# Windowed attention and a four-expert layer on one core: steps ordered by a list scheduler, gate logits turned back by transposes

## The chip, the cores and the metric

The kernel runs on one core of a Trainium2 chip. A core has five engines that work side by side and wait for one another by semaphores: TensorE (PE in the profile; its weight loads are PEld), VectorE (DVE), ScalarE (ACT), GpSimd (POOL) and SyncE (SP), which here only starts DMA transfers. Each engine works through its own queue in the order of the program. The metric is device time in microseconds, the median of several runs; less is better.

## The reference

Eight batches of 576 positions. First a symmetric sliding-window attention with 8 heads of width 64, then a layer of four causal attention experts, of which each position uses the best two.

```
scores = q @ k.T / sqrt(64), kept where |i - j| <= 32
x = softmax(scores) @ v                      # heads side by side: 576 x 512
logits = x @ w_gate                          # 576 x 4
top 2 of 4, w = softmax over these two
for e in 4 experts:
    a = causal softmax((x @ wq[e]) @ (x @ wk[e]).T / sqrt(64))
    out += w[e] * (a @ (x @ wv[e]) @ wo[e])  # where e is among the two
```

## The kernel before

The work of a batch is cut into steps, each a Python function that issues a handful of instructions; all loops are unrolled. A window group `g` is four of the eight heads, so a batch has two groups.

- `load_qk`, `load_v`: DMAs from SP's queue. Per group 0.59 MB (576 KB) each of k and q; per batch 1.18 MB of v, and then two copies inside the chip (lines 94 and 95, 0.92 MB in all) that make a second, shifted layout of v. These copies wait in SP's queue until v has landed.
- `turn(b, g, nm)` (line 207): VectorE transposes k or q of a group, two instructions.
- `win_scores(b, g, half)` (228): 40 small fp32 products on TensorE into two PSUM tiles, then an exp on ScalarE (234) and a product with the mask (236), on VectorE in batch 0 and on GpSimd later.
- `win_av` (264) multiplies by v for a pair of heads, and ScalarE copies the result (268). `win_sums` (243) makes the softmax sums of a batch, and five VectorE instructions (248 to 253) invert them into `RS`. `win_norm` (279 to 283) spreads `RS` by four products, VectorE multiplies (281, tile XTF), GpSimd casts (283, tile XTB).
- `moe_gate1` (299, 302), `moe_gate2` (304 to 326) and `moe_gate3` (331 to 337): the gate. TensorE leaves the logits as partial sums in `GT`, in four groups of 32 rows; `moe_gate2` multiplies 128 columns of `GT` by a selection matrix `SELG`, which adds the four groups and turns the result, so that positions lie on partitions, in tile `pl`.
- `moe_proj_qk` (349, out by ScalarE at 354 for q and VectorE at 356 for k), `moe_proj_v` (371), `moe_scores(b, j, c)` (391, exp at 394, causal mask on GpSimd at 398 to 405), `moe_av` (417, VectorE 424 to 426), `moe_turn` (439), `moe_y` (450, ScalarE 455, DMA 457 and 459). Experts go in two pairs `j`; a pair's scores come in four chunks `c`.

PSUM has eight banks: three tiles of two banks (`slot`), which nearly all steps share, and two of one bank (`slot1`) for `sums`, `pl` and `pt`. SBUF tiles rotate as well: three of each of `kn` and `qn`, two of `vsb`, three of `AT` (the window weights of a group), one of `XTF` and `XTB`.

What sets the order is the table `ORDER`, written out by hand and run once per batch in a software pipeline: `N` steps work for the next batch but one round (loads, first turns), `W` for the batch of this round (window scores), `M` for the batch before it (all the rest up to the experts' products) and `Z` for the one before that (second pair's product, output). The program keeps this order on each engine.

## Time and profile before

| | |
|---|---|
| median of 3 runs | 350.93 us (347.72 to 351.21) |
| profiled execution, its own time | 351.94 us |
| its span, first to last instruction | 350.2 us |
| mean granted TensorE clock | 0.924 of full |
| busy: PE, PEld, DVE, ACT, POOL | 279.6, 206.9, 190.4, 148.6, 131.9 us |
| DMA | 48.00 MB, mean 137 GB/s |

The profiled execution's own time is 1.74 us above its span. In the rows further down a line such as `[12.37 <-DVE QKE L356]` says that the engine was idle 12.37 us before the instruction and that a VectorE instruction of line 356, which wrote tile QKE, ended that wait.

### The profile page before, as it was taken

Reading aid. Unit: us, or ns where it says so; the run is one execution under the profiler, and the core shown is the slowest. Engines: PE = TensorE matmul, PEld = TensorE weight load, DVE = VectorE, ACT = ScalarE, POOL = GpSimd, SP = SyncE. Lnnn points to the kernel's source line nnn. Section 1 sums busy time; section 2 is a strip of 40 time slices with the busy share of each in tenths; the row PEclk is TensorE's granted clock in tenths of the full one; section 3 lists DMA queues with packets and bytes.
Section 4 is the critical chain, followed back from the end, with each engine's and each line's share of the span. In section 5 each row is a group of like instructions: output and inputs, shape, how many; then the busy total and the mean of one; then the engine's idle time right before and its main releaser. Section 6 shows DMA issues by size and latency. Waiting matters only on the chain.

```text
span 350.2 us, 12556 instructions
## 1 busy us (share of the span) xinstructions
PE 279.6 (80%) x5672; PEld 206.9 (59%) x5680; DVE 190.4 (54%) x380; ACT 148.6 (42%) x224; POOL 131.9 (38%) x186
## 2 busy tenths in 40 slices
PE   0878609887997899797988798879979898869864
PEld 0766406576576756585757655766658566744541
DVE  7976035638483558537573749274853743370440
ACT  1235503441646255623554175515562266415332
POOL 7002700443348055615354354614561534530110
PEclk9999955798999999998999999998999699998886
DMA  7997897800588039720957077803972030003003
GB/s 283 221 220 189 150 303 184 232 4 2 184 225 236 10 127 266 142 118 3 321 120 211 4 247 179 226 2 135 264 154 101 2 137 2 4 2 135 2 1 135
DMA packets 58181, 48.00 MB, mean 137 GB/s; under 512 B 45584, under 2 KB 45584, under 8 KB 58128
## 3 DMA queue, kind: packets, MB, share of 16 engines
q1 hardware_dynamic: 58128, 47.20, 49.4%
q8 instruction: 44, 0.72, 0.9%
q14 instruction: 9, 0.07, 0.1%
HBM read 30.42 MB, written 9.44 MB: 114 GB/s over the span
## 4 chain that ended last, share of the span: by engine, by line
PE 62%; DVE 15%; ACT 9%; DMA 5%; SPq 4%; issue 3%; ACTq 0%; POOL 0%; POOLq 0%; DVEq 0%
PE sc L228 13%; PE u L264 9%; PE pp L349 8%; PE po L417 7%; PE py L450 7%; ACT ATE L394 5%; PE pv L371 5%; PE sums L243 4%; DVE XTF L281 4%; ACT AT L234 4%; DVE Tkn L207 3%; DMA kn<-in_k_dram 3%; PE pl L308 3%; PE ps L391 3%; PE pg L299 2%
## 5 line engine op out<-in xcount | busy, mean ns | idle before, releaser
L236 POOL TENSOR_TENSOR AT<-AT,MASKP 128x576 f32<-128x576 f32 x56 | 77.8, 1411 | 65.0 <-ACT AT L234 65.0
L228 PE MATMUL sc<-Tqn,Tkn 32*64 32x128 f32 (+3 forms) x2560 | 60.2, 302 | 19.0 <-DVE Tqn L207 8.3
L234 ACT ACTIVATE AT<-sc 128x576 f32<-128x576 f32 x64 | 38.2, 648 | 86.9 <-PE sc L228 86.9
L228 PEld LDWEIGHTS sc<-Tqn,Tkn 32*64 32x64 f32 x2560 | 50.4, 150 | 29.6 <-DVE Tqn L207 8.8
L394 ACT ACTIVATE ATE<-ps 128x1024 bf16<-128x1024 f32 x64 | 51.0, 836 | 36.1 <-PE ps L391 35.9
L283 POOL CAST XTB<-XTF 128x576 bf16<-128x576 f32 x32 | 21.3, 668 | 89.6 <-DVE XTF L281 89.6
L264 PE MATMUL u<-AT,vsb 128*64 128x64 f32 (+1 forms) x1024 | 39.2, 236 | 8.8 <-ACT ATE L394 6.8
L207 DVE STREAM_TRANSPOSE Tkn<-kn 128x576 f32<-128x576 f32 x32 | 37.3, 1240 | 15.4 <-DMA kn<-in_k_dram 15.4
L264 PEld LDWEIGHTS u<-AT,vsb 128*64 128x64 f32 x1024 | 35.5, 143 | 12.1 <-ACT ATE L394 7.6
L268 ACT COPY us<-u 128x576 f32<-128x576 f32 x32 | 20.5, 639 | 41.0 <-PE u L264 41.0
L207 DVE STREAM_TRANSPOSE Tqn<-qn 128x576 f32<-128x576 f32 x32 | 37.2, 1240 | 0.0
L391 PE MATMUL ps<-QKE 64*128 64x512 bf16 (+2 forms) x192 | 22.2, 290 | 16.9 <-DVE QKE L356 14.1
L356 DVE CAST QKE<-pp 128x576 bf16<-128x576 f32 x16 | 12.0, 747 | 43.0 <-PE pp L349 43.0
L398 POOL TENSOR_SCALAR_AFFINE_SELECT ATE<-ATE 128x384 bf16<-128x384 bf16 x32 | 16.0, 523 | 48.7 <-ACT ATE L394 48.7
L417 PE MATMUL po<-VE,ATE 128*128 128x65 bf16 (+2 forms) x480 | 27.1, 198 | 2.0 <-POOL ATE L398 1.6
L424 DVE RECIPROCAL po<-po 128x8 f32<-128x8 f32 (+1 forms) x32 | 6.2, 194 | 39.0 <-PE po L417 38.4
L455 ACT COPY ysb<-py 128x1024 f32<-128x1024 f32 (+1 forms) x24 | 19.6, 873 | 18.4 <-PE py L450 9.9
L450 PE MATMUL py<-WO,OTT 128*128 128x512 bf16 (+1 forms) x72 | 24.1, 461 | 3.2 <-DVE OTT L441 2.0
L417 PEld LDWEIGHTS <-ATE 128*128 128x128 bf16 (+2 forms) x480 | 21.4, 101 | 7.8 <-POOL ATE L398 1.7
L248 DVE RECIPROCAL sums<-sums 128x144 f32<-128x144 f32 x8 | 8.5, 1067 | 30.0 <-PE sums L243 30.0
L371 PE MATMUL pv<-WV,XTB 128*128 128x256 bf16 (+1 forms) x160 | 22.4, 292 | 2.4 <-ACT AT L234 2.4
L391 PEld LDWEIGHTS <-QKE 64*128 64x128 bf16 x192 | 7.0, 96 | 27.0 <-DVE QKE L356 15.1
(72 smaller groups left out, 333.2 us busy)
## 6 DMA issues: line engine op xcount, KB each, us to landing
kn<-in_k_dram SPq DMA_DIRECT2D x16, 576.0 KB, 6.3
qn<-in_q_dram SPq DMA_DIRECT2D x16, 576.0 KB, 6.9
vsb<-in_v_dram SPq DMA_DIRECT2D x32, 256.0 KB, 7.0
out_dram<-ysb SPq DMA_DIRECT2D x16, 512.0 KB, 2.9
vsb<-vsb SPq DMA_DIRECT2D x8, 512.0 KB, 5.1
vsb<-vsb SPq DMA_DIRECT2D x8, 384.0 KB, 7.0
vsb<-in_v_dram SPq DMA_DIRECT2D x8, 128.0 KB, 4.5
out_dram<-ysb SPq DMA_DIRECT2D x8, 128.0 KB, 3.4
```

Source lines behind the costliest of these rows:

```text
L207: nc.vector.transpose(T[:, dh, :].rearrange("p (t s) -> p s t", s=18), n_[:, :, 32 * dh:32 * dh + 32])
L228: nc.tensor.matmul(sl[hh // 2][64 * par:64 * par + 64, hh % 2, lo - c0:hi - c0], KT[r, dh, k0:k0 + 64], QT[r, dh, lo:hi], start=(dh == 0), ...
L234: nc.scalar.activation(ap, sl[p][:, :, 0:HS], EXP, scale=scale_att)
L236: eng.tensor_tensor(out=ap, in0=ap, in1=MASK[:, None, c0:c0 + HS].to_broadcast([128, 2, HS]), op=MULT)
L264: nc.tensor.matmul(u[64 * x:64 * x + 64, half, lo - HS * half:hi - HS * half], V[:, c, h, :], A[:, h % 4, lo:hi], start=True, stop=True, s ...
L283: nc.gpsimd.tensor_copy(XTB[:, pair, :], XTF[:, pair, :])
L349: nc.tensor.matmul(pp[:, half, 0:HS], WQK[j][n][:, dt, :], XTB[:, dt, HS * half:HS * half + HS], start=(dt == 0), stop=(dt == NDT - 1))
L371: nc.tensor.matmul(o, XTB[:, dt, 128 * t:128 * t + n], WV[:, dt, :], start=(dt == 0), stop=(dt == NDT - 1))
L391: nc.tensor.matmul(ps[0:rows, eo, at:at + hi - lo], QKE[r, 1, 128 * kt:128 * kt + nrow(kt)], QKE[r, 0, lo:hi], start=True, stop=True)
L394: nc.scalar.activation(ATE[0:rows, :, 512 * c:512 * c + w], ps[0:rows, :, 0:w], EXP, scale=scale_moe)
L417: nc.tensor.matmul(po[0:n, eo, 65 * qt:65 * qt + 65], ATE[0:nk, eo, o:o + n], VE[0:nk, kt, 2 * j + eo, :], start=(kt == 0), stop=(kt == qt))
L450: nc.tensor.matmul(py[0:n, t - t0, :], OTT[:, j, 128 * t:128 * t + n], WO[:, j, :], start=(j == 0), stop=(j == 1))
```

## The change

The hand-written table goes. In its place every step of all eight batches is declared with its engine costs, its predecessors (data and buffer reuse) and the PSUM tiles that it takes (`D` of the wide ones, `S` of the narrow). `way` is the longest way from a step to the end. A greedy loop keeps a clock per engine and repeatedly takes, of the steps whose predecessors are placed, the one with the smallest start time less 0.06 times its `way`; a step without TensorE work is placed as soon as its start is due. The program then issues the steps in that order. `load_qk` is split so that k and q are loaded by separate steps. In `moe_gate2` the five products with `SELG` become five fp32 transposes of `GT` into a wide PSUM tile `ptr`, and two VectorE reductions add the four groups.

```diff
-    def load_qk(b, g):
-        for nm, src in (("kn", k), ("qn", q)):
+    def load(b, g, nm):
+        for src in ({"kn": k, "qn": q}[nm],):
...
     def moe_gate2(b):
         sh = [128, NQT, 4]
+        ptr = slot("ptr")
+        for t in range(NQT):
+            nc.tensor.transpose(ptr[:, t // 4, 128 * (t % 4):128 * (t % 4) + 128],
+                                GT[:, 128 * t:128 * t + 128], ident)
         pl = slot1("pl")
-        for t in range(NQT):
-            nc.tensor.matmul(pl[:, 4 * t:4 * t + 4], GT[:, 128 * t:128 * t + 128], SELG,
-                             start=True, stop=True)
+        nc.vector.tensor_reduce(pl[:, 0:16].rearrange("p (t e) -> p t e", e=4),
+                                ptr[:, 0, :].rearrange("p (t d e) -> p t e d", d=4, e=32)[:, :, 0:4, :],
+                                axis=AXX, op=ADD)
+        nc.vector.tensor_reduce(pl[:, 16:20],
+                                ptr[:, 1, 0:128].rearrange("p (d e) -> p e d", e=32)[:, 0:4, :],
+                                axis=AXX, op=ADD)
...
-    ORDER = """
-        M win_av 0 | M win_av 1 | M win_sums | M win_av 2 | M win_av 3 | Z moe_av 1
...
-        M moe_gate1 | M moe_proj_qk 0 0 | M moe_proj_qk 0 1 | W turn 1 qn
...
-    """
+                if i > 2:
+                    step(("load", i, nm), lambda b=b, g=g, nm=nm: load(b, g, nm), 0,
+                         [("turn", i - 3, nm)], then=[("DMA", 1.6), ("LAT", 2.0)])
...
+        else:
+            step(("load_v", b), lambda: None, 0, [], then=[("LAT", 14.0)])
...
+        step(("G2", b), lambda b=b: moe_gate2(b), 0.55, [("G1", b)] + ([("G3", b - 1)] if b else []), D=1, S=1,
+             then=[("DVE", 1.7)])
...
+    def way(n):
+        if n not in tail:
+            s_ = steps[n]
+            tail[n] = s_["pe"] + sum(c + 0.2 for _, c in s_["then"]) + max([way(u) for u in users[n]], default=0)
+        return tail[n]
...
+    while left:
+        cand = [(try_step(n), n) for n in left if all(a in done for a in left[n]["after"])]
+        now = free["PE"]
+        best = None
+        for t, n in cand:
+            if not left[n]["pe"]:
+                ok = t <= now + 0.3
+                key = (0 if ok else 1, t if not ok else -way(n))
+            else:
+                key = (1, max(t, now) - SLACK * way(n) * 0.01)
+            if best is None or key < best[0]:
+                best = (key, t, n)
...
     with tc.manual_schedule():
-        load_qk(1, 0)
+        load(1, 0, "kn")
+        load(1, 0, "qn")
         load_weights(0)
...
+        for n in order:
+            steps[n]["fn"]()
+            if n == ("turn", 1, "qn"):
+                spread_sel(0)
```

What this makes of the order is shown at three places. The first is ScalarE's queue in batch 0, where the tiles `sc` are the window scores and `u` the products with v, in the order in which TensorE makes them. Before:

```order
L234 ACTIVATE AT_239<-sc0_294 128x2x288
L234 ACTIVATE AT_239<-sc1_295 128x2x288
L234 ACTIVATE AT_340<-sc0_341 128x2x288
L234 ACTIVATE AT_340<-sc1_342 128x2x288
L234 ACTIVATE AT_340<-sc0_391 128x2x288
L234 ACTIVATE AT_340<-sc1_392 128x2x288
L268 COPY us_454<-u_437 128x576
L268 COPY us_473<-u_456 128x576
```

After:

```order
L230 ACTIVATE AT_218<-sc0_267 128x2x288
L230 ACTIVATE AT_218<-sc1_268 128x2x288
L264 COPY us_340<-u_323 128x576
L264 COPY us_362<-u_345 128x576
L230 ACTIVATE AT_368<-sc0_369 128x2x288
L230 ACTIVATE AT_368<-sc1_370 128x2x288
L230 ACTIVATE AT_368<-sc0_415 128x2x288
L230 ACTIVATE AT_368<-sc1_416 128x2x288
```

The first group's two products with v (`us_340`, `us_362`) now stand ahead of the second group's scores (`AT_368`).

The second is SP's queue after the weights (`tmpw`, `tmpv` and `tmpo` are the experts' weights); `kn_387` and `qn_389` before are k and q of batch 1, group 1, and so are `kn_265` and `qn_313` after. Before:

```order
L179 DMA tmpv_216<-in_moe_wv_dram 128x4x64 x4
L183 DMA tmpo_221<-in_moe_wo_dram 64x512 x4
L90 DMA vsb_286<-in_v_dram 128x8x64 x4
L92 DMA vsb_286<-in_v_dram 64x8x64
L94 DMA vsb_286<-vsb_286 64x4x512
L95 DMA vsb_286<-vsb_286 64x3x512
L82 DMA kn_387<-in_k_dram 128x1152
L82 DMA qn_389<-in_q_dram 128x1152
L82 DMA kn_646<-in_k_dram 128x1152
```

After:

```order
L175 DMA tmpv_202<-in_moe_wv_dram 128x4x64 x4
L179 DMA tmpo_207<-in_moe_wo_dram 64x512 x4
L83 DMA kn_265<-in_k_dram 128x1152
L83 DMA qn_313<-in_q_dram 128x1152
L91 DMA vsb_315<-in_v_dram 128x8x64 x4
L93 DMA vsb_315<-in_v_dram 64x8x64
L95 DMA vsb_315<-vsb_315 64x4x512
L96 DMA vsb_315<-vsb_315 64x3x512
L83 DMA kn_461<-in_k_dram 128x1152
L83 DMA qn_463<-in_q_dram 128x1152
L83 DMA kn_569<-in_k_dram 128x1152
```

The k and q of that group now stand ahead of v of batch 1 (`vsb_315`) and its two copies; behind these come batch 2's `kn_461`, `qn_463` and `kn_569`.

The third is VectorE's queue where batch 1 is normalised. Before:

```order
L281 TENSOR_TENSOR XTF_1157<-us_1018,rb_1159 128x576
L281 TENSOR_TENSOR XTF_1157<-us_1037,rb_1166 128x576
L441 COPY OTT_1173<-pt_1174 128x576
L281 TENSOR_TENSOR XTF_1157<-us_1097,rb_1181 128x576
L281 TENSOR_TENSOR XTF_1157<-us_1116,rb_1188 128x576
L441 COPY OTT_1173<-pt_1195 128x576
L207 STREAM_TRANSPOSE Tkn_1202<-kn_887 128x18x32 x2
```

After:

```order
L381 CAST VE_659<-pv_1007 64x4x64
L203 STREAM_TRANSPOSE Tqn_1051<-qn_657 128x18x32 x2
L277 TENSOR_TENSOR XTF_1108<-us_817,rb_1110 128x576
L203 STREAM_TRANSPOSE Tkn_1169<-kn_679 128x18x32 x2
L277 TENSOR_TENSOR XTF_1108<-us_839,rb_1178 128x576
L203 STREAM_TRANSPOSE Tqn_1190<-qn_788 128x18x32 x2
L277 TENSOR_TENSOR XTF_1108<-us_1030,rb_1239 128x576
L203 STREAM_TRANSPOSE Tkn_1312<-kn_890 128x18x32 x2
L277 TENSOR_TENSOR XTF_1108<-us_1049,rb_1315 128x576
```

The four multiplications into `XTF_1108` now stand with one turn of a later group (batch 2 and 3) between each two; before, only the short copies `OTT` stood between.

Named as batch, group or pair, and part, TensorE's order after begins: both score halves of group 0, two products with v, scores of group 1, sums, two products with v, four `win_norm`, then q of pair 0, scores, v, q of pair 1, scores, scores of batch 1 group 1, k of pair 0, and so on; the first expert product with v of batch 0 (`moe_av`) comes after the scores of batch 3's second group have begun. At the end, the output steps of batches 4 to 6 stand among the projections, scores and products of batches 6 and 7.

## Rows read from the trace of the kernel before

**Rows 1.** The page's first part: busy time, share of the span, instructions.

```profile
PE 279.6 (80%) x5672; PEld 206.9 (59%) x5680; DVE 190.4 (54%) x380; ACT 148.6 (42%) x224; POOL 131.9 (38%) x186
```

**Rows 2.** Windows of the program's start: length, busy by engine, TensorE clock, DMA share, GB/s.

```profile
0.00:9.14 9.14, 0.84 (x16) 0.33 (x16) 6.83 (x14) 1.49 (x2) 6.54 (x26) 1.00 0.80 283
9.14:23.01 13.87, 10.45 (x308) 9.03 (x309) 11.15 (x16) 4.77 (x8) 0.00 (x0) 1.00 0.99 227
23.01:41.70 18.69, 15.99 (x396) 13.18 (x396) 9.41 (x13) 10.04 (x16) 5.95 (x7) 1.00 0.85 176
41.70:52.80 11.10, 0.00 (x0) 0.00 (x0) 2.98 (x4) 0.00 (x0) 2.36 (x3) 0.63 0.95 277
52.80:66.50 13.70, 13.70 (x140) 9.02 (x140) 8.21 (x18) 4.06 (x6) 1.60 (x4) 0.56 0.85 191
66.50:91.93 25.43, 21.20 (x479) 15.94 (x478) 13.71 (x28) 11.43 (x17) 12.55 (x14) 0.93 0.12 44
```

**Rows 3.** Timeline of the start: start us, us, engine, line, operation, wait before it.

```profile
23.01 3.79 PE L264 MATMUL u<-AT,vsb 128*64 128x64 f32 x60 [1.84 <-DMA vsb<-vsb]
29.29 1.07 DVE L248 RECIPROCAL sums<-sums 128x144 f32<-128x144 f32 x1 [2.04 <-PE sums L243]
31.48 0.36 DVE L253 SCALAR_TENSOR_TENSOR RS<-Hb,NM,sums 128x144 bf16<-128x144 bf16 x1
32.43 2.75 DVE L281 TENSOR_TENSOR XTF<-us,rb 128x576 f32<-128x576 f32 x4 [0.59 <-PE rb L279]
36.98 1.16 PE L349 MATMUL pp<-XTB,WQ 128*128 128x288 bf16 x8
42.30 2.24 SPq L82 DMA_DIRECT2D kn<-in_k_dram  x1
49.83 2.34 DVE L207 STREAM_TRANSPOSE Tkn<-kn 128x576 f32<-128x576 f32 x2 [14.65 <-DMA kn<-in_k_dram]
52.01 0.74 DVE L356 CAST QKE<-pp 128x576 bf16<-128x576 f32 x1
52.80 0.61 PE L391 MATMUL ps<-QKE 64*128 64x512 bf16 x2 [12.37 <-DVE QKE L356]
```

**Rows 4.** Windows of five periods and of the end, columns as in the second group.

```profile
91.93:128.71 36.78, 31.86 (x711) 24.02 (x711) 22.64 (x45) 17.78 (x28) 16.95 (x21) 1.00 0.56 155
...
242.24:281.96 39.72, 34.97 (x711) 25.68 (x712) 22.65 (x45) 17.95 (x27) 17.03 (x21) 0.91 0.55 151
281.96:319.37 37.41, 31.23 (x630) 22.77 (x632) 16.10 (x39) 16.76 (x25) 14.39 (x20) 0.95 0.10 35
319.37:350.20 30.83, 20.90 (x166) 12.46 (x166) 8.84 (x28) 10.84 (x15) 3.19 (x8) 0.80 0.17 61
```

**Rows 5.** Timeline of TensorE in one period.

```profile
113.58 2.17 PE L243 MATMUL sums<-AT,OH 128*32 128x144 f32 x64
115.67 2.28 PE L264 MATMUL u<-AT,vsb 128*64 128x96 f32 x64
117.89 1.67 PE L417 MATMUL po<-VE,ATE 128*128 128x65 bf16 x30
...
120.00 0.52 PE L439 MATMUL pt<-ident_bf,OE 128*128 128x128 bf16 x5
...
125.22 2.45 PE L450 MATMUL py<-WO,OTT 128*128 128x512 bf16 x9
127.60 1.18 PE L299 MATMUL pg<-XTF,WG 128*32 128x288 f32 x16
...
130.77 1.39 PE L228 MATMUL sc<-Tqn,Tkn 32*64 32x64 f32 x80
...
132.88 1.91 PE L371 MATMUL pv<-WV,XTB 128*128 128x256 bf16 x16 [0.40 <-ACT AT L234]
...
135.04 1.28 PE L308 MATMUL pl<-SELG,GT 128*128 128x4 f32 x10
...
148.21 0.30 PE L264 MATMUL u<-AT,vsb 128*64 128x96 f32 x2 [0.97 <-ACT ATE L394]
```

More of the change, by code (lines that the diff above doesn't have):

```diff
@@ L20 @@
 PE = mybir.EngineType.PE
+SLACK = 6.0
 S = 576
@@ L96, in load_v @@
         vsb[b] = t
-    load_qk(0, 0)
-    load_qk(0, 1)
+    for g in range(2):
+        for nm in ("kn", "qn"):
+            load(0, g, nm)
     load_v(0)
@@ L481, with step @@
[L481 to L486 removed]
+    steps = {}
+    def step(name, fn, pe, after, D=0, S=0, then=()):
+        steps[name] = dict(fn=fn, pe=pe, after=list(after), D=D, S=S, then=list(then))
@@ new lines @@
+    tail = {}
+    users = {n: [] for n in steps}
+    for n, s_ in steps.items():
+        for a in s_["after"]:
+            users[a].append(n)
+    def way(n):
[3 more added lines that the diff above has]
+        return tail[n]
+    import sys
+    sys.setrecursionlimit(20000)
+    LATE = 0.2
+    free = dict(PE=7.0, ACT=3.0, DVE=4.0, POOL=6.0, DMA=10.0)
+    ring = {"D": [0.0] * 3, "S": [0.0] * 2}
@@ new lines, with try_step @@
+    done, order = {}, []
+    left = dict(steps)
+    def try_step(n):
+        s_ = left[n]
+        t0 = max([done[a] for a in s_["after"]], default=0.0) + LATE
+        for r in "DS":
+            if s_[r]:
+                t0 = max(t0, ring[r][s_[r] - 1] + LATE)
+        if s_["pe"]:
+            return max(t0, free["PE"])
+        return max(t0, free[s_["then"][0][0]] if s_["then"][0][0] in free else 0.0)
+    while left:
[10 more added lines that the diff above has]
+                best = (key, t, n)
+        _, t, n = best
+        s_ = left.pop(n)
+        order.append(n)
+        end = t + s_["pe"]
+        if s_["pe"]:
+            free["PE"] = end
+        x = end
+        rel = []
+        for e_, c in s_["then"]:
+            if e_ == "LAT":
+                x += c
+                continue
+            x = max(x + LATE, free[e_]) + c
+            free[e_] = x
+            if e_ in ("ACT", "DVE"):
+                rel.append(x)
+            if n[0] == "S" and e_ == "ACT":
+                x = end
+        if n[0] == "S":
+            x = max(free[e_] for e_, _ in s_["then"])
+        done[n] = x
+        for r in "DS":
+            for q_ in range(s_[r]):
+                ring[r] = ring[r][1:] + [(rel[min(q_, len(rel) - 1)] if r == "D" and n[0] == "S" else
+                                          max(rel) if rel else end)]
```

109 lines of the change are left out of this document (63 added, 46 removed).

## The prediction

> **What bounds the kernel now.** First the page's busy times: TensorE works 279.6 of 350.2 us (80%), VectorE 54%, the others less than half the time [rows 1]. So TensorE is the engine to fill, and the questions are where its 70 idle us lie, and where its clock is low. The windows answer both. In the start [rows 2] it is idle 8.3 us, then 13.87 - 10.45 = 3.4, then 2.7, then the whole of 41.70 to 52.80 (11.1), then 4.2 up to 91.93. In five like periods it is idle between 36.78 - 31.86 = 4.9 and 39.72 - 34.97 = 4.75 us, about 5 each [rows 4]. The end, from 281.96, is idle 6.2 + 9.9 = 16.1 us in 68.2. The clock column stands at 1.00 or a little below nearly everywhere; after the 11 us hole it is 0.56 (that is, mostly at the lower level, 1.2 instead of 2.4 GHz), and 0.80 in the last 31 us.
>
> The timeline explains the hole [rows 3]. k of batch 1, group 1 is issued by SP at 42.30, behind v and its two copies. VectorE takes its turn of it at 49.83 after 14.65 us of waiting, and the cast of QKE that stands behind that turn runs at 52.01; TensorE needs QKE and had waited 12.37 us. In a period the waits are small and spread [rows 5]: 0.97 us for the last exp of the scores, 0.40 for an exp whose PSUM tile is wanted.
>
> **The change, part by part.** The sum is made against the profiled span of 350.2.
>
> *Start, to the first projection.* SP's queue is the same up to the weights, so v's copies again free the product with v at 23.01, and 3.79 us of it follow [rows 3]. Before, the scores of group 1 filled that wait; now they stand behind it (the first place shown of the order). That puts 2 x 1.39 = 2.8 us of scores [rows 5] and, at an estimate of 1.4, their last exp and mask (each is like the 0.69 us of one multiplication in the row at 32.43) on the path: +4.2. A turn of k, 2.34, now stands on VectorE ahead of the first XTF: +2.3. The last XTF ended at 32.43 + 2.75 = 35.2 and would end at 41.7; with the cast on GpSimd, again 0.7, the first projection starts at 42.4 instead of 36.98. Without these scores TensorE is also idle for 3.4 + 2.8 = 6 us or more before 23, most of it in one piece, and after the 11 us hole the clock was 0.56 for 13.7 us [rows 2]. Bounds for that: nothing (8.3 idle us at the very start left the clock at 1.00 in the next window) and +7 (9 us of work, three quarters longer). I take +3, as most of this work is small products that wait for one another: 45.4.
>
> *The hole.* Now k and q of batch 1, group 1 stand ahead of v (the second place). Up to them 8.9 MB are to be moved, and the windows give 283 x 9.14 + 227 x 13.87 + 176 x 18.69 = 9.0 MB by 41.7 [rows 2]: both have landed before their turns. Up to q of batch 2, group 0 it is 12.2 MB; with 277 x 11.1 more, 12.1 MB by 52.8, and its turns come later. So the hole goes and so does the low clock behind it. What is late next is VectorE: from 45.4 it has five turns of 2.34 and two casts, 13.7 us, beside TensorE's 16.5 us up to the scores of batch 2 (five halves of 1.39, four projections of 1.0 to 1.16, V 1.91, two products with v 2.28, gate 1.18). With 2 us of waits that ends near 64.
>
> *The crowded stretch.* Then the third place: VectorE does six turns (14.0), two chains of sums (29.29 to 31.84, 2.55 each), four XTF (2.75) and a cast, 22.3 us, in strict alternation, while TensorE has some 17 us of work. The stretch lasts at least 22.3; with waits I take 26 (to 32). The first projection of batch 1 starts near 90, against 91.93: -1.9. By then TensorE has done more on one side (four score halves 5.6, two products with v 2.3, sums 2.17) and less on the other (gate 1.18, two expert products 2 x 1.67, two turns 1.04, output 2.45, the first `moe_gate2` 0.6, a chunk 0.2): ahead by 1.2. Start in all: **-3.1** (-11 to +7).
>
> *Gate.* Five products with `SELG` took 1.28 us [rows 5]. The trace has no fp32 transpose. From below, five bf16 transposes took 0.52 [rows 5]; from above, if each fp32 transpose went in four passes where the product went in two, 2 x 1.28 = 2.6. I take 0.6, the nearest row in kind, a gain of 0.65 for each of 7 batches of which some lies beside waits: **-4** (-5 to +9). The two reductions add about 0.9 us a batch on VectorE (the larger reads 512 columns, the XTF row has 576 in 0.69), which is busy 22.6 of 37 us in a period [rows 4]; the gate's result is wanted only by `moe_av`, many steps later. That cover gone, it would cost 0.9 x 8 = 7.
>
> The Trainium skill, TensorE: Matmul & The Clock Gate, Part 4: PE-mode transpose, puts a bf16 transpose of 128x128 at about 275 ns in one kernel; five in a row took 0.52 us here, 0.1 each, since they overlap, so the trace does not agree. By that figure, as an estimate, the gate would take 1.4 us and the sum would be 4 us higher.
>
> *Middle.* From batch 1's projections to the end TensorE has the same steps left but for the two terms above. `ptr` takes one of the three wide PSUM tiles once more per batch. I price that like the wait of 0.40 for an exp [rows 5], six times: **+2.4**. Otherwise I leave the 5 us of idle per period: the order takes away the waits in the rows (something else stands behind `moe_av` and `moe_scores`), and makes others, as it sets steps with little TensorE work (`win_norm`, score chunks, output) side by side, each of which needs its tile emptied by ScalarE or VectorE. Bounds -10 to +15.
>
> *End.* Before, batch 7 ran nearly alone. Now output steps of batches 4 to 6 and the products of 6 stand between its steps. At the rate of a full period (5 idle in 37) 68 us would hold 9 of idle, against 16.1; and the clock at 0.80 should rise. The last chain, product, OE, turn, output, copy, DMA, stays. **-9**: 7 from idle, 2 from the clock (-4 to -13).
>
> Sum: 350.2 - 3.1 - 4 + 2.4 - 9 = 336.5. The profiled time is 1.74 above its span and the median 1.01 below the profiled time: 337 us.
>
> **The rivals.** *The middle closes too.* If the order also removes a third of the 5 us in six periods (-10) and `ptr` costs nothing, 336.5 - 12.4 + 0.7 = 325. For it: the waits there are short and the engines far from full. Against: TensorE is at 87% there already.
>
> *The tiles in PSUM set the pace.* Three wide tiles serve every step, and order adds none. With 2.5 us more of idle per period in place of 0.4, six times, the span is 349, the time 350: no change. For it: both waits, of 0.40 and 0.97, end with an exp that empties such a tile. The Trainium skill, Perfetto Trace Analysis, Identifying Performance Opportunities, says that the same gap repeating on the engine that should be saturated can mean that buffers ran out; the repeated 0.97 us agrees, and by that rule a new order alone would leave the middle as it is or move its gaps.
>
> *Slower.* XTF now alternates with turns on VectorE in later batches too. Each XTF empties a wide tile, and one stuck behind a turn of 2.34 us holds TensorE's next steps. In batches 2 to 7 there are 24; at 1 us each the span is 336.5 + 24, the time 361. It decides from 0.57 us each (13.7 / 24). For it: 22.3 us of VectorE in the crowded stretch. Against: each turn replaces one that stood elsewhere, and VectorE is idle 14 us a period.
>
> *The transposes are not cheaper.* At 2.4 instead of 0.6 us in eight batches: +14, 352, no change. Against it: the instruction is marked as a transpose, not as a product.
>
> **How the numbers follow.** Forecast 0.55, centred on 337 and reaching from 330 to 345; middle closes 0.19; tiles 0.12; slower 0.09; transposes 0.05. 1% is 3.5 us, about what a measurement of this kernel, whose three runs lie 3.5 us apart, can tell from no change. Faster by more than that (below 347.4): 0.55 + 0.19 and a share of the two cases near 350, 0.78; same 0.11; slower 0.11. A range of 323 to 349 leaves out the slower case, some of the cases at 350, and the far end of the second: 0.2.
>
> **What would show it.** Right: the first projection between 42 and 46, no hole of over 5 us after it, the first projection of batch 1 near 90, `ptr` at 0.6 us per five, idle of 4 to 6 us per 37 in the middle and 9 or less in the last 68. Wrong: turns that wait for loads between 60 and 90; TensorE waiting for XTF in every batch; a clock below 0.9 through the middle, which no term here has.

## The result and the profile after

The changed kernel takes 321.18 us (median of 4 runs, 318.32 to 322.47), the kernel before 351.07 beside it (347.72 to 351.84): ratio 0.916, 95% interval 0.909 to 0.923. The direction was foreseen; the size was not: 321 lies below the range of 323 to 349. The profiled execution has a span of 319.6 us at a mean granted clock of 0.961 of full, against 350.2 and 0.924. The kernel before ran between 340.17 and 353.09 us in all the sets of runs here, beside the later runs mostly near 347, and its profiled execution (351.94) is among the long ones, so that a difference read from its trace can be some 4 us larger than one of medians.

The page's first part, to be read beside [rows 1]:

```profile
PE 265.4 (83%) x5640; PEld 197.2 (62%) x5640; DVE 196.1 (61%) x395; ACT 148.7 (47%) x224; POOL 130.8 (41%) x182
```

TensorE's busy time fell by 279.6 - 265.4 = 14.2 us and its idle time by 70.6 - 54.2 = 16.4. Nearly the same instructions are issued, so a fall of 14 in busy time already says that something other than waits was gained. One row of the page's list of DMA queues matters further down: DMA also brings the instructions themselves, in 44 packets (0.72 MB, so 16 KB each).

```profile
q8 instruction: 44, 0.72, 0.9%
```

The windows of the kernel after, columns as in [rows 2]:

```profile
21.29:38.50 17.21, 12.92 (x364) 11.06 (x365) 9.37 (x15) 8.90 (x14) 0.67 (x1) 1.00 0.85 222
38.50:63.80 25.30, 22.33 (x593) 16.89 (x594) 17.31 (x17) 9.17 (x15) 14.90 (x14) 0.87 0.82 201
63.80:91.08 27.28, 20.70 (x556) 16.32 (x555) 17.96 (x21) 12.60 (x18) 16.91 (x19) 0.81 0.91 253
91.08:251.40 160.32, 145.46 (x3277) 110.82 (x3276) 104.98 (x224) 78.75 (x121) 78.98 (x97) 0.98 0.45 123
251.40:319.60 68.20, 58.27 (x691) 37.58 (x690) 31.73 (x98) 35.41 (x51) 13.45 (x32) 0.99 0.29 105
```

The last line is the end: idle 68.20 - 58.27 = 9.9 us in the last 68, at a clock of 0.99. The one above it is the middle: 14.9 us idle in 160.3. The same two stretches before:

```profile
91.93:282.00 190.07, 165.38 (x3547) 124.17 (x3552) 113.22 (x225) 89.22 (x136) 85.31 (x105) 0.96 0.55 152
282.00:350.20 68.20, 52.08 (x794) 35.20 (x795) 24.94 (x67) 27.60 (x40) 17.58 (x28) 0.89 0.13 47
```

There the middle was idle 24.7 us at a clock of 0.96, the end 16.1 at 0.89.

The start, timeline of all engines after; it answers to [rows 3]:

```profile
21.29 3.73 PE L260 MATMUL u<-AT,vsb 128*64 128x64 f32 x60 [6.68 <-DMA vsb<-vsb]
...
38.50 0.42 PE L353 MATMUL pp<-XTB,WQ 128*128 128x288 bf16 x1
...
71.32 2.34 DVE L203 STREAM_TRANSPOSE Tqn<-qn 128x576 f32<-128x576 f32 x2 [4.55 <-DMA qn<-in_q_dram]
...
72.73 0.58 PE L224 MATMUL sc<-Tqn,Tkn 32*64 32x96 f32 x4 [1.64 <-DVE Tqn L203]
...
91.08 1.15 PE L353 MATMUL pp<-XTB,WQ 128*128 128x288 bf16 x8
```

The first projection starts at 38.50 (36.98 before), that of batch 1 at 91.08 (91.86 before; the windows of [rows 4] begin at 91.93). The wait of 12.37 us is gone; the longest now is the 6.68 for v's copies. So the start is worth 0.8 us, and everything else lies behind 91 us.

TensorE after, while batch 3 is normalised (`rb` is `win_norm`, `u` the products with v, the first two shown of batch 3, the others of batch 4):

```profile
134.24 0.42 PE L275 MATMUL rb<-RS,SEL 128*128 128x144 bf16 x4
135.03 1.25 PE L260 MATMUL u<-AT,vsb 128*64 128x96 f32 x32 [0.36 <-ACT AT L230]
136.21 1.39 PE L224 MATMUL sc<-Tqn,Tkn 32*64 32x64 f32 x80
137.53 1.25 PE L260 MATMUL u<-AT,vsb 128*64 128x96 f32 x32
138.71 0.42 PE L275 MATMUL rb<-RS,SEL 128*128 128x144 bf16 x4
139.06 1.25 PE L260 MATMUL u<-AT,vsb 128*64 128x96 f32 x32
140.25 0.42 PE L275 MATMUL rb<-RS,SEL 128*128 128x144 bf16 x4
```

And the same step before, twice, one period apart; all but the last of these rows stand in the gap of [rows 5], and the prediction did not use them:

```profile
119.49 0.67 PE L279 MATMUL rb<-RS,SEL 128*128 128x144 bf16 x8
...
121.56 0.42 PE L279 MATMUL rb<-RS,SEL 128*128 128x144 bf16 x4 [1.05 <-DVE OE L426]
122.22 0.41 PE L279 MATMUL rb<-RS,SEL 128*128 128x144 bf16 x4 [0.23 <-DVE XTF L281]
...
123.91 1.37 PE L228 MATMUL sc<-Tqn,Tkn 32*64 32x96 f32 x76 [0.62 <-DVE XTF L281]
...
160.76 2.30 PE L228 MATMUL sc<-Tqn,Tkn 32*64 32x96 f32 x76 [0.62 <-DVE XTF L281]
```

Before, four spreading steps and two output turns stand together. They are short for TensorE (0.1 to 0.5 us each), and all need VectorE, which has 2.75 us of XTF and the OE instructions to do: waits of 1.05, 0.23 and 0.62, 1.90 of the 4.9 idle us of the period. In the second period the same 76 score products take 2.30 instead of 1.37 us: behind the same waits the clock has fallen (0.96 in that period, 1.00 in the one before it). After, each spreading step has 1.2 us or more of TensorE work behind it, and VectorE is mostly done by the next: one wait for XTF is left, of 0.72 us at 142.88.

TensorE's waits for these two tiles over the whole middle, in us in total, times and longest, from the view of waits; before:

```profile
PE rb L279 <- DVE OE L426: 5.2, 5, 1.1
PE sc L228 <- DVE XTF L281: 2.5, 4, 0.6
PE rb L279 <- DVE XTF L281: 1.2, 5, 0.2
```

After, its two largest:

```profile
PE rb L275 <- DVE OE L430: 1.3, 2, 0.7
PE sc L224 <- DVE XTF L277: 1.0, 2, 0.7
```

In all, waits for OE and XTF fell from 8.9 to 2.9 us. Those for the exp of the expert scores (ATE), among them the 0.97 us of [rows 5], fell too, from 9.9 to 4.5; against that stand 2.6 us of waits that the middle did not have before.

The gate after, from the groups by line (busy, mean ns, idle before):

```profile
L304 PE MATMUL ptr<-ident,GT 128*128 128x128 f32 x40 | 6.3, 284 | 0.9 <-ACT ATE L398 0.5 <-issue 0.4
```

Five transposes in a row take 0.77 us (the row at 277.98; the next instruction starts 0.89 later, others 0.65 to 0.70) against the 1.28 of [rows 5].

### The profile page after: what moved, and what is told of

Read it like the earlier page. It is cut to its first block, busy times and chain, and to the rows that moved or that the text cites. A ratio compares the mean times of both kernels' runs of the same rounds, so it can differ in the third digit from the quotient of the medians.

```text
span 319.6 us, 12489 instructions
## 1 busy us (share of the span) xinstructions
PE 265.4 (83%) x5640; PEld 197.2 (62%) x5640; DVE 196.1 (61%) x395; ACT 148.7 (47%) x224; POOL 130.8 (41%) x182
## 4 chain that ended last, share of the span: by engine, by line
PE 45%; ACT 11%; DVE 4%; issue 2%; DMA 1%; ACTq 0%; DVEq 0%
PE pp L353 8%; PE sc L224 7%; PE po L421 7%; PE u L260 6%; ACT ATE L398 5%; PE py L454 4%; PE pv L375 4%; PE sums L239 3%; ACT AT L230 2%; ACT ysb L459 2%; PE pg L295 2%; PE ps L395 1%; PE pt L443 1%; DMA out_dram<-ysb 1%; PE ptr L304 1%
## 5 line engine op out<-in xcount | busy, mean ns | idle before, releaser
L224 PE MATMUL sc<-Tqn,Tkn 32*64 32x128 f32 (+3 forms) x2560 | 54.8, 296 | 17.5 <-DVE Tqn L203 9.7
L224 PEld LDWEIGHTS sc<-Tqn,Tkn 32*64 32x64 f32 x2560 | 47.3, 147 | 26.3 <-DVE Tqn L203 8.1
L398 ACT ACTIVATE ATE<-ps 128x1024 bf16<-128x1024 f32 (+1 forms) x64 | 51.4, 838 | 18.2 <-PE ps L395 18.2
L260 PE MATMUL u<-AT,vsb 128*64 128x64 f32 (+1 forms) x1024 | 43.2, 240 | 10.6 <-DMA vsb<-vsb 6.7
L260 PEld LDWEIGHTS u<-AT,vsb 128*64 128x64 f32 x1024 | 37.2, 146 | 15.6 <-issue 10.0
L277 DVE TENSOR_TENSOR XTF<-us,rb 128x576 f32<-128x576 f32 x32 | 23.8, 750 | 24.1 <-PE rb L275 20.7
L395 PE MATMUL ps<-QKE 64*128 64x320 bf16 (+5 forms) x192 | 22.1, 288 | 6.0 <-ACT ATE L398 3.3
L454 PE MATMUL py<-WO,OTT 128*128 128x512 bf16 (+1 forms) x80 | 21.0, 381 | 1.9 <-ACT ATE L398 1.0
L375 PE MATMUL pv<-WV,XTB 128*128 128x256 bf16 (+1 forms) x160 | 20.8, 278 | 1.1 <-ACT ATE L398 0.8
L353 PE MATMUL pp<-XTB,WQ 128*128 128x288 bf16 x128 | 19.8, 295 | 1.5 <-POOL XTB L279 0.8
L428 DVE RECIPROCAL po<-po 128x8 f32<-128x8 f32 (+1 forms) x32 | 6.2, 194 | 24.1 <-PE po L421 21.2
```

The lines of the kernel that those rows point to most:

```text
L224: nc.tensor.matmul(sl[hh // 2][64 * par:64 * par + 64, hh % 2, lo - c0:hi - c0], KT[r, dh, k0:k0 + 64], QT[r, dh, lo:hi], start=(dh == 0), ...
L260: nc.tensor.matmul(u[64 * x:64 * x + 64, half, lo - HS * half:hi - HS * half], V[:, c, h, :], A[:, h % 4, lo:hi], start=True, stop=True, s ...
L353: nc.tensor.matmul(pp[:, half, 0:HS], WQK[j][n][:, dt, :], XTB[:, dt, HS * half:HS * half + HS], start=(dt == 0), stop=(dt == NDT - 1))
L375: nc.tensor.matmul(o, XTB[:, dt, 128 * t:128 * t + n], WV[:, dt, :], start=(dt == 0), stop=(dt == NDT - 1))
L395: nc.tensor.matmul(ps[0:rows, eo, at:at + hi - lo], QKE[r, 1, 128 * kt:128 * kt + nrow(kt)], QKE[r, 0, lo:hi], start=True, stop=True)
L398: nc.scalar.activation(ATE[0:rows, :, 512 * c:512 * c + w], ps[0:rows, :, 0:w], EXP, scale=scale_moe)
```

## The experiments

My theory after the result had two parts: the gain of the middle comes from the order around `win_norm`, and the gain of the end from steps that were held back. The rivals: load order, the gate, a scheduler whose numbers happen to fit. Each time stands against the kernel before on the same chip.

**The gate undone in the new order, and alone in the old.** In the first kernel the five products with `SELG` are back in the kernel after, in the second the transposes are put into the kernel before:

```diff
-            nc.tensor.transpose(ptr[:, t // 4, 128 * (t % 4):128 * (t % 4) + 128],
-                                GT[:, 128 * t:128 * t + 128], ident)
+            nc.tensor.matmul(pl[:, 4 * t:4 * t + 4], GT[:, 128 * t:128 * t + 128], SELG,
+                              start=True, stop=True)
```

> The changed kernel with the five products with SELG put back in place of the five transposes and the two reductions; the order of all steps is the same, instruction for instruction, but for these. Theory A (the order makes the gain, the gate is a small term): the product takes 1.21 us from start to start and the transposes 0.69, so TensorE gets 0.52 us more per batch, 4 us in eight, while VectorE and one wide PSUM tile get free: 322 to 326 us. Theory B (the gate carries a third or more of the 30 us, since it also frees TensorE's neighbours): 331 us or more.

> The kernel before with the transposes and reductions in its gate and nothing else. Theory A: at most the 0.52 us per batch of TensorE, less what the extra wide PSUM tile costs in the fixed order, where the gate stands between score chunks: 346 to 351 us. Theory B: 341 us or less.

Measured: 329.78 (329.16 to 335.21; ratio 0.951, 0.944 to 0.957) for the first and 345.95 against 347.06 (0.9995, 0.995 to 1.004) for the second. So the gate is worth nothing that can be measured in the old order and some 9 us in the new one. In the profiled execution of the first kernel the span is 8.7 us longer than that of the kernel after, and about half of it is one place of TensorE's timeline:

```profile
158.25 0.46 PE L418 MATMUL po<-VE,ATE 128*64 128x65 bf16 x5 [1.35 <-issue]
160.51 1.87 PE L451 MATMUL py<-WO,OTT 128*128 128x512 bf16 x4
162.17 2.52 PE L418 MATMUL po<-VE,ATE 128*128 128x65 bf16 x30
```

A wait of 1.35 us in the middle of an expert product, with no releaser in the trace, and then every instruction at little over half speed (1.87 for a `py` that takes 1.04, 2.52 for a `po` of 1.67). Another 2.0 us arise in its start, where v's copies end TensorE's wait at 23.32 and not at 21.29; no gate has run by then. To see whether it comes back, both kernels were run again.

> The changed kernel itself, so that the three others of this call stand beside it on one chip. 316 to 322 us.

> The changed kernel with the products with SELG, once more, beside the changed kernel on one chip. Theory A (the gate costs TensorE 0.52 us per batch and nothing more; the rest of the first measurement was the start and one fall of the clock): 4 to 6 us over the changed kernel. Theory B (with the new order the gate stands on the path and carries a third of the gain): 9 us or more over it.

Measured: 319.67 (318.62 to 321.31; ratio 0.922, 0.917 to 0.928) and 329.19 (324.71 to 332.95; 0.949, 0.939 to 0.956). The medians repeat. The profiled execution of the second was its fastest: it has the same wait without a releaser (1.20 us, at 154.94), this time with one slow `po` behind it (2.33 us at 158.13), and its span is 322.9 against 319.3. The products are busy 10.1 us in it, the transposes 6.1 in the other: these 4.0 us are the gate's own. The four executions of the second lie 5.0 to 13.3 us above the median of the first.

The packed traces, which hold the time of every DMA packet and instruction, say what the waits without a releaser are. Over all 16 profiles 49 waits of TensorE of 0.35 us or more have none. If TensorE's instructions are counted in order, 46 of them lie whole multiples of 256 instructions apart (40 exactly, the others with up to five more or less, and some records can be missing from a trace), and end 1.2 to 1.7 us after a packet of `q8 instruction` has landed, of 16 KB or 64 bytes for each of 256. So TensorE waits there for the next block of its own program, where that comes late. They sum to 9.2 us in the profile of the first kernel and 4.8 in that of the second, against 3.5 and 3.3 in the two of the kernel after, and none is that long in the kernel before. So beside the products' own 4 us the traces show late blocks, the low clock behind them and, in the first kernel, a load that came late. These are not to be added up (5.7 us more of late blocks, 2.0 for the load and 4.5 for the products would be more than the 8.7 of the first profile), since some of it falls into other waits. Why blocks come late more often in these executions, and whether the gate has a part in it, no run here shows.

**Loads first.** The kernel before, with k and q of batch 1, group 1 issued ahead of v of batch 1, as the new order has it:

```diff
+                if i == 0 and fn == "load_v":
+                    load_qk(1, 1)
```

> The kernel before with one move: k and q of batch 1, group 1 are issued ahead of v of batch 1, as in the changed kernel's queue. Theory A (the hole of 11 us in the start comes from that place in the queue alone, and the low clock behind it goes with it): the hole shrinks to under 3 us and the time falls by 8 to 13 us, to 338 to 343. Rival (the start is bound by the bytes, so the wait only moves to v or to the next k): under 4 us gained, 347 or more.

Measured: 342.44 (341.5 to 346.68), ratio 0.987 (0.980 to 0.994). The wait of 12.37 us is gone, but this one stands a few steps further on:

```profile
54.52 2.30 PE L228 MATMUL sc<-Tqn,Tkn 32*64 32x96 f32 x76 [7.20 <-DVE VE L377]
```

The gain of 4.6 lies between the two expectations. So the hole is a small part of the 26 to 30 us.

**Scores between the spreading steps.** The kernel before, with the next batch's first score half moved up, to keep TensorE at work while VectorE does XTF:

```diff
-        M win_norm 0 | M win_norm 1 | Z moe_turn 0 | M win_norm 2 | M win_norm 3 | Z moe_turn 1
-        W turn 1 kn | W win_scores 0 0
+        M win_norm 0 | M win_norm 1 | W win_scores 0 0 | Z moe_turn 0 | M win_norm 2 | M win_norm 3 | Z moe_turn 1
+        W turn 1 kn
```

> The kernel before with one move in its table: the first score half of the next batch is issued between the second and third win_norm of a batch instead of behind all four and the turn. Theory C (in the middle the run of four win_norm, two turns and their waits for VectorE leaves TensorE idle 3 to 4 us in 5 and lets its clock fall in some periods; steps with much TensorE work among them take both away): idle per period falls from 5 to 3.5 us, the clock rises to 0.99 or 1.00 in all periods, the time falls by 8 to 14 us, to 337 to 343. Rival (the middle is held by the three wide PSUM tiles, so the wait moves to the next step that needs one): period unchanged within 0.5 us, 348 or more.

Measured: 355.97 (349.32 to 362.07), ratio 1.015 (1.001 to 1.028): no faster, and rather slower, by less than the runs of this kernel differ. The timeline of TensorE (of the run of 357.61) says why nothing was gained:

```profile
120.47 0.67 PE L279 MATMUL rb<-RS,SEL 128*128 128x144 bf16 x8
122.64 2.87 PE L228 MATMUL sc<-Tqn,Tkn 32*64 32x96 f32 x80 [1.49 <-DVE OE L426]
```

Scores take two wide PSUM tiles. Two are still held by `rb` until VectorE gets to their XTF, and the third by the expert product until OE is done. The wait only moved, and my remedy fell. What I took from it is that the work to stand there should need one tile only, emptied by another engine; the edit further down tries that.

**The scheduler's weight.** The kernel after with the weight of the longest way at 0, so that the earliest start wins, and at 10:

```diff
-SLACK = 6.0
+SLACK = 0.0
```

> The changed kernel's planner with the weight of the longest way set from 6 to 0, so that it takes the step that can start first. Theory: the priority by the longest way is what keeps the pipeline between batches at an even depth; without it the steps of late batches run ahead and the end is bare: 330 us or more. Rival: any order that looks at when a step can start fills the gaps as well: within 4 us of the changed kernel.

> The kernel after, with the weight of the longest way in the scheduler's choice at 10 in place of 6; at 0 the time was 344.9, at 6 it was 320. Theory: the gain comes from taking work with a long way behind it early, and most of it is had at 6, since TensorE then is busy 265 of 320 us and the rest lies at the start and the end, so 10 gives 316 to 323 (ratio 0.91 to 0.93). Rival: the weight has an optimum near 6, since at 10 a step is taken although its start lies up to a tenth of its way ahead, and TensorE then waits for it; 325 or more (ratio above 0.935).

Measured: 344.88 (342.64 to 348.99; ratio 0.992, 0.988 to 0.997) at 0, 324.99 (323.75 to 328.8; 0.934) at 10, beside 319.67 (0.922) and 321.18 (0.916) at 6. So the loads, the split of k and q, the gate and a greedy packing without the priority bring together about 1%, and the priority carries some 25 us. At 10 the kernel is 4 to 5 us slower than at 6, on another chip: that is the rival's number, and 6 may lie near the best weight. Windows of the middle and the end at 0:

```profile
95.43:273.10 177.67, 157.32 (x3367) 116.89 (x3371) 107.61 (x227) 86.42 (x131) 78.33 (x98) 0.97 0.47 129
273.10:341.30 68.20, 54.03 (x738) 34.75 (x738) 27.78 (x74) 29.37 (x42) 18.30 (x31) 0.86 0.15 53
```

The end is again 14.2 us idle at a clock of 0.86, much like that of the kernel before. But the waits of the middle for OE and XTF are 3.5 us here, nearly as few as at 6 (2.9): the spreading steps stand apart in this order too. Of the 21.7 us by which its span exceeds that of the kernel after, 4.4 arise by the start of the middle, 9.7 are idle and 7.6 busy time of middle and end. So the priority is not what takes the spreading steps apart; what it gains lies in other waits, the end and the clock.

**A wrong cost corrected.** The scheduler believes v of batch 0 to be there at 14 us; the trace has it at 21 to 23. With 23 in its table:

> The changed kernel with one number of the planner's table corrected: the first v is there at 23 us, as in both traces, and not at 14. Then the scores of group 1 go ahead of the products with v again. Theory (the wait of 6.7 us for v's copies with scores behind it costs time to the end): 3 to 6 us faster than the changed kernel. Rival (the start is bound by bytes and by VectorE later on, which absorb it): within 2 us.

Measured: 324.89 (322.49 to 325.29; ratio 0.935), 5 us slower than the kernel after. It reorders more than the start, and gets a worse stretch between 40 and 90 us: a product with v at 52.84 waits 4.12 us for the copies of batch 1's v, and the gate of batch 1 starts 5.8 us later than in the kernel after (103.62 against 97.84). A truer number in a greedy planner is no promise of a better order.

**Alternation by hand.** The kernel before with two lines of its table changed, nothing else; the sums also move to the front:

```diff
-        M win_av 0 | M win_av 1 | M win_sums | M win_av 2 | M win_av 3 | Z moe_av 1
-        M win_norm 0 | M win_norm 1 | Z moe_turn 0 | M win_norm 2 | M win_norm 3 | Z moe_turn 1
+        M win_sums | M win_av 0 | M win_av 1 | M win_norm 0 | M win_av 2 | M win_norm 1 | M win_av 3
+        Z moe_av 1 | M win_norm 2 | Z moe_turn 0 | M win_norm 3 | Z moe_turn 1
```

> The kernel before, with its table changed in two lines: the sums stand first, and each spreading step of the window branch (its wide PSUM tile is emptied by VectorE) stands between two products with v (emptied by ScalarE) or output products, where the four stood side by side in pairs. Theory of alternation: what closed the middle is that steps which wait for one engine to empty their tile no longer stand side by side; idle per period falls from 5 to about 3 us, the time to 335 to 342 against 347 (ratio 0.965 to 0.985). Rival, tiles: three wide tiles serve every step, so the wait moves on to the next step that needs one, as when the scores were set between; 344 or more (ratio above 0.99).

Measured: 336.15 (335.09 to 339.06) against 347.30, ratio 0.969 (0.961 to 0.978). The timeline of TensorE in one period and, below, the windows of its five periods:

```profile
144.94 0.41 PE L279 MATMUL rb<-RS,SEL 128*128 128x144 bf16 x4 [0.45 <-DVE RS L253]
145.28 1.25 PE L264 MATMUL u<-AT,vsb 128*64 128x96 f32 x32
146.46 0.42 PE L279 MATMUL rb<-RS,SEL 128*128 128x144 bf16 x4
146.81 1.25 PE L264 MATMUL u<-AT,vsb 128*64 128x96 f32 x32
148.00 1.67 PE L417 MATMUL po<-VE,ATE 128*128 128x65 bf16 x30
149.60 0.42 PE L279 MATMUL rb<-RS,SEL 128*128 128x144 bf16 x4
```

```profile
86.00:121.60 35.60, 32.45 (x711) 24.30 (x712) 22.83 (x45) 17.72 (x27) 17.05 (x22) 1.00 0.58 161
121.60:157.20 35.60, 32.46 (x711) 24.31 (x712) 22.81 (x45) 17.72 (x27) 17.06 (x22) 1.00 0.58 161
157.20:194.96 37.76, 32.79 (x711) 24.34 (x712) 22.83 (x45) 17.72 (x27) 17.08 (x22) 1.00 0.55 152
194.96:230.50 35.54, 32.40 (x711) 24.26 (x712) 22.82 (x45) 17.69 (x27) 17.01 (x22) 1.00 0.59 161
230.50:267.50 37.00, 32.83 (x715) 24.38 (x712) 22.83 (x45) 17.75 (x28) 17.12 (x22) 1.00 0.56 156
```

The waits for XTF are nearly gone, of those for OE 0.23 and 0.31 us remain in a period, and one of 0.45 for RS is new; three of five periods have 3.1 us of idle instead of 4.9, 18.6 in all. The other two (5.0 and 4.2) hold a wait for a late block of the program, of 1.83 us at 179.33 and 1.04 at 251.40. And the clock is 1.00 in all five, where the kernel before had 1.00, 0.96, 1.00, 0.96 and 0.91 with 24.7 us of idle. Per period that is up to 1.8 us from waits and, where the clock had fallen, 0.6 to 2.1 from the clock (34.97 us busy at 0.91 in [rows 4] against 32.83 here). Two things were changed at once: over the five periods the waits for OE and XTF fall from 8.9 to 2.9 us, which is the alternation, and those for ATE from 9.9 to 5.0, which comes with the sums, since they now stand in the place of the products with v that waited 0.97 us a period. The two were not tried apart.

**Alternation forbidden in the new order.** The kernel after, each `win_norm` only behind all four products with v of its batch:

```diff
-                     [("U", i, x), ("SUM", b)] +
+                     [("U", 2 * b + g_, x_) for g_ in range(2) for x_ in range(2)] + [("SUM", b)] +
```

> The kernel after, with its scheduler made to place the spreading steps of a batch only behind all four products with v of that batch, so that they can no longer alternate with these; it may still set scores, projections and output steps between them. Theory of alternation: the idle of the middle comes back in part, 326 or more against 320 (ratio to the kernel before above 0.94). Rival, it is the freedom to set any step of any batch beside them, by the longest way, that matters and not these two kinds: the scheduler finds other work, 318 to 323 (ratio 0.915 to 0.932).

Measured: 334.72 (331.6 to 335.82; ratio 0.962, 0.955 to 0.970). The number is the theory's; the trace only in part. Of the 10.2 us by which its span exceeds that of the kernel after, 8.9 have arisen by the gate of batch 1 (107.12 against 98.24), in the crowded stretch:

```profile
66.12 0.45 PE L239 MATMUL sums<-AT,OH 128*32 128x144 f32 x6 [1.87 <-issue]
...
75.03 1.50 PE L224 MATMUL sc<-Tqn,Tkn 32*64 32x64 f32 x80 [2.48 <-DVE VE L381]
```

From there to the gate of batch 6 it needs 172.05 us, the kernel after 168.21. Yet the waits that the theory names are back in its middle:

```profile
PE po L421 <- DVE OE L430: 3.0, 3, 1.1
PE sc L224 <- DVE XTF L277: 2.2, 2, 1.9
```

With the smaller ones they are 7.9 us, against 2.9 in the kernel after and 8.9 in the kernel before. So the pairing does carry these waits, and it is worth some 4 us of the middle. Most of the 13 us of this run arose in the crowded stretch, and so its time does not separate the theories as I had meant it to.

**Both hand-made edits, and with the gate.** The kernel before with alternation and loads first; then with the transposes as well:

> The kernel before with both edits of its hand-made order: the alternation of the spreading steps (alone 336.15, -11.1) and the loads of k and q of batch 1, group 1 ahead of v (alone 342.4, -4.6). Theory: the two act in different places, periods and start, so they add, 330 to 333 against 347 (ratio 0.950 to 0.962); what is left to 320 is then the end, which both leave alone (68 us with about 14 idle at a clock of 0.89). Rival: both gains came from the same low clock behind the hole of batch 1, so together they give little more than the alternation alone: 335 or more (ratio above 0.965).

> The hand-made order with both edits (alternation and loads first, 334.8) and the gate's transposes as well. In the old order the transposes brought nothing (345.95 against 347.06), in the new one 9.5 us by medians. Theory: they count once the order leaves TensorE few waits to hide them in; here the idle of a period is 3.6 instead of 5 us, so most of 8 x 0.6 = 4.8 us arrives, 329 to 332. Rival: with the products, the new order has an event of its own (a stall and a low clock behind it) that no hand-made order has; then they bring nothing here either, 333.5 to 336.

Measured: 334.81 (333.52 to 337.35) against 346.59 (ratio 0.982, 0.966 to 0.998, where the medians alone give 0.966; it is wide because the kernel before itself ran between 340.17 and 352.76 there); and 329.40 (327.59 to 331.10) against 349.02 (0.951, 0.940 to 0.961). By medians the loads add 1.3 us to the alternation, not 4.6: nearer to the rival, and no more than runs differ. The profiled executions, split at the starts of two gate products in the timelines (that of the kernel before is its long one):

| us to the gate of batch 1, from there to that of batch 6, to the end | | | |
|---|---|---|---|
| before | 90.75 | 190.03 | 69.42 |
| loads first | 84.42 | 187.29 | 68.09 |
| alternation | 84.82 | 181.48 | 68.40 |
| both | 80.10 | 183.42 | 68.28 |
| both, and the gate | 82.67 | 178.68 | 66.75 |

The alternation gains 8.5 us in the five periods and 5.9 in the start. The transposes, worth nothing in the old order, bring 5.4 us here by medians (of two chips), 4.7 of it in the five periods of the profiles. But that is not time which the gate saved: a period without a disturbance takes 35.6 us with the products and 35.7 with the transposes, since the steps behind them now wait 0.30 and 0.28 us for VectorE's VE. The five periods of *both* hold a fall of the clock (0.95 in a period of 36.94) and two late blocks of the program (1.91 and 1.58 us); those of the last row hold no fall of the clock and only 0.36 and 0.35 us of such blocks. Theory and rival are both left open by this: the medians fit the theory, the trace does not show it. The ends of all five stay within 3 us of one another.

**No lead.** The kernel after, with the sums of a batch placed only behind the last output step of the batch two before it, as the table had it:

```diff
+             + ([("Y", b - 2, 4)] if b > 1 else [])
```

> The kernel after, with its scheduler made to place the sums of a batch only behind the last output step of the batch two before it, as the hand-made table did; the window branch can no longer run ahead of the output. Theory of the end: the output steps that were held back are what fills the last 68 us; without them the idle there goes from 9.9 back towards 14 to 16 us and its clock from 0.99 towards 0.9, and the time is 328 to 335. Rival: any order that goes by the longest way packs as well, and the lead is a by-product; 318 to 324.

Measured: 324.20 (322.13 to 325.74; ratio 0.936, 0.927 to 0.945), 3.0 and 4.5 us above the two medians of the kernel after, on the rival's edge. Windows of the middle and the end:

```profile
90.00:255.80 165.80, 146.19 (x3311) 108.32 (x3315) 106.75 (x213) 84.52 (x127) 78.04 (x98) 1.00 0.52 142
255.80:324.00 68.20, 57.18 (x773) 38.55 (x768) 30.36 (x89) 29.71 (x44) 18.23 (x32) 0.91 0.15 53
```

The clock of the end falls from 0.99 to 0.91, as the theory had it, but its idle time only rises from 9.9 to 11.0. The lead of the window branch is worth some 3 to 4 us in all; the rest of the end's gain is there without it, in this order by the longest way.

## Why the prediction was right and wrong

**Start (-3.1): small and right in kind.** It was worth 0.8 by the first projection of batch 1 (91.08, foretold 90). The first projection came at 38.50, not 45.4: v's copies freed TensorE at 21.29 instead of 23.01 (21.02 to 23.53 in the other profiles of orders made by the scheduler, so this part is chance), the projection starts on the first piece of XTB instead of the last (pieces up to 40.56), and the low clock (+3) added nothing: the 60 products with v take 3.73 us, before 3.79, and the 84 scores behind them 1.47. The bound of nothing for it rested on a 1.00 of the clock column in [rows 2] that is no reading: the trace before has no record of the clock up to 27.42, and there 80 scores took 2.98 us at 14.84, against 1.39 in [rows 5]. TensorE was at the lower level in the start of both kernels. The hole went. The crowded stretch was as long as foretold (63.80 to 91.08: 27.3 us, foretold 26), with the turns that wait for loads that were named as a sign of being wrong (4.55 us at 71.32). Tried alone in the old order, the loads bring 4.6 us.

**Gate (-4): right for TensorE's own time.** The five transposes take 0.77 us and free TensorE after 0.65 to 0.89, foretold 0.6. Eight times 0.5 is 4 us, and the traces of the new order show 10.1 us for the products and 6.1 for the transposes. Whole executions differ by more, 9.5 by medians, and for the rest the traces show late blocks of the program, the clock behind them and a late load; that the gate causes them is not shown. Not foreseen: in the old order it is worth nothing, where it shortened a step with waits beside it. The Trainium skill's figure of about 275 ns for one bf16 transpose (TensorE: Matmul & The Clock Gate, Part 4: PE-mode transpose) is near the row's mean of 284 ns for one in fp32. In a row they overlap, so that five take 0.77 us and not 1.4; the prediction held that figure against a fifth of a row of five, where the groups by line before have 236 ns for one bf16 transpose (`pt`).

**Middle (+2.4): the step that failed.** The prediction left "the 5 us of idle per period" in place and added a price for `ptr`; measured were -9.8 us of idle there (24.7 to 14.9), what the rival *the middle closes too* had as -10, with 0.19. Two things went wrong in it. It quoted the waits of 0.97 and 0.40 from [rows 5] and passed over 1.90 us of others in the same period, all in one place. And it took the new order to "set steps with little TensorE work side by side", where the kernel before did that and the new order takes them apart. The runs show this cause for 6 of the 9.8 us: waits for OE and XTF fell from 8.9 to 2.9 us in the middle; the two lines changed by hand take as many of them from the kernel before; and where the scheduler may not pair the spreading steps with the products with v they are back at 7.9. The kernel changed by hand is 11 us faster in all, with the sums moved and the start shorter as well. The waits for ATE, whose 0.97 the prediction had quoted and left in place, account for 5.4 more, of which 2.6 went into new waits. The priority has no part in taking the steps apart: at a weight of 0 these waits are 3.5 us, though that kernel loses 25.

**Clock: no term in the middle.** From the first projection of batch 1 on, TensorE's busy time fell from 217.46 to 203.73 us. Of the 13.7, seven gates at 0.52 are 3.6 and the work ahead 1.2 by the prediction's own count; what is left, 8.9, is the same work at a higher clock, where the prediction had 2, for the end. The records of the granted clock bear it out: in these stretches TensorE was busy 24.1 us at the lower level before and 6.6 after. If that work takes half as long at the higher one, the 17.4 us between them are worth 8.7; by the 76 scores, which took 2.30 and 1.37 us, 7.0 (estimates from these rows). It read the clock as "1.00 or a little below nearly everywhere" and gave the 0.91 and 0.95 of [rows 4] no price.

**End (-9): right.** Idle fell from 16.1 to 9.9 us (foretold 9) and the clock rose from 0.89 to 0.99. Held-back output steps stand there as foretold; that they are the whole cause is not so: without the lead 11.0 us of idle remain.

**The other rivals.** *The tiles set the pace* was half true: moved scores wait for tiles, and that kernel is no faster, but products with v, of one tile that ScalarE empties, fit in. *Slower by XTF behind turns* fell: in the whole kernel after, the groups by line put 2.3 us of the window scores' waits and 0.6 of the experts' scores' down to XTF, where it needed 13.7. The Trainium skill's rule that repeated gaps can mean too few buffers (Perfetto Trace Analysis, Identifying Performance Opportunities) did not decide this case: with the same three wide tiles the middle lost 9.8 us of its gaps.

The sum mended: 336.5, less 12.2 (the middle's idle, -9.8 for +2.4), less 6.9 (the clock), plus 1.1 by which the start, 0.8 by which the idle of the end and 0.4 by which seven gates fell short, is 319.7, against a span of 319.6. It closes by its making, since the clock's share is what was left over; the check on it is the 7.0 to 8.7 above.

Open: how the last 8 us between the best hand-made order (329.4) and the new one divide. The lead is some 3 to 4. Which waits the priority removes, one by one. And why blocks of the program came late more often in the profiles with the products than in those with the transposes.

## What to carry to other kernels

List the waits of a whole period before a price is put on any, and look for where they stand together: short steps that one engine must empty, set side by side, make that engine set the pace of the stretch; put between them steps that need one tile and another engine. Where idle time goes, price the granted clock as well, by periods of the same work at both levels (36.8 and 39.7 us in [rows 4]). And an edit that saves half a microsecond of a busy engine needs several executions and a look at its periods: by medians the transposes brought 0 us in one order, 5 in another and 9 in a third, while the traces show at most the 4 of TensorE's own time, and in the second order none of it.

## What the hardware showed that was not expected

Behind the same short waits the clock falls in one period and not in the next: behind 1.05, 0.23 and 0.62 us the 76 score products took 1.37 us at 123.91 and 2.30 at 160.76. Seven runs of the kernel before on one chip went from 344.69 us at a granted clock of 0.942 to 349.65 at 0.933, so a hundredth of clock goes with as much as some edits bring, though not strictly (347.30 stands at 0.942 too); in the kernel after the two go together less well (318.32 at 0.978, 318.62 at 0.952).

TensorE also waits for its own program. It stops inside a step, mostly with no releaser in the trace (1.50 us at 69.32 in the kernel after, 1.35 and 1.20 above, 1.87 at 66.12, up to 2.88 at a weight of 10), and the instructions behind such a stop can run at the lower level. The stops come at one place in its queue, a multiple of 256 instructions apart, and end shortly after a 16 KB packet of the instruction queue has landed: in the kernel after at 55.86, 69.32 and 154.50 us, with packets that ended at 54.70, 67.80 and 153.08. In an unrolled kernel this is a cost of its own, 3.3 to 9.2 us in the profiles of the new order with either gate. The view of waits can give such a stop another name: the 1.83 us in the alternated order stand there as a wait for GpSimd (`POOL ATE`), at the same place of a block and 1.4 us behind a packet.
